# Joining the attention result by transfers and a GpSimd addition, with one low half fewer per other block, in a fused attention and two-layer kernel

## The chip, the cores and the metric

One core of one Trainium2 chip runs one program. The metric is device microseconds (us) of one execution; the figure for a kernel is the median of its runs. TensorE (PE, with PEld for its weight loads) multiplies matrices, VectorE (DVE), ScalarE (ACT) and GpSimd (POOL) work on tiles, and SyncE (SP) issues nearly all DMA transfers.

## The reference

Attention is limited by hash buckets: with B = 2, H = 8, S = 768, D = 64, a score counts only where the six sign bits of `q @ proj` and `k @ proj` agree.

```python
mask = q_bucket[:, :, :, None] == k_bucket[:, :, None, :]
scores = np.where(mask, scale * np.matmul(q, k.transpose(0, 1, 3, 2)), -1e9)
attn = np.exp(scores - np.max(scores, axis=-1, keepdims=True))
attn = attn / (np.sum(attn, axis=-1, keepdims=True) + 1e-09)
x = np.matmul(attn, v)                 # to (1536, 512)
h = x @ w_in;  g = h * np.tanh(softplus(h));  x = g @ w_out      # 512 -> 2048 -> 512
h = x @ w2_in; g = h - np.tanh(h);            out = g @ w2_out
```

## The kernel before, in words

The arithmetic is float32. For each product the kernel splits an operand into a rounded high half and a low half (value minus high) and multiplies high by high, low by high and high by low.

Every piece of work is an `op` with an engine, a modelled cost and a key. `Plan.order` simulates all of them on modelled engines (ready operations by key) and writes out one fixed order for each engine; SP's DMA issues are ordered in the same way (engine "DMA"). The chip then runs each engine's list in order, with semaphores between the engines. All constants `AT_*`, `TICK`, `JIT`, `TOK_T`, `LATG` enter keys and modelled latencies only, so they change the order and nothing else.

**Attention** takes the eight head pairs g = 0 to 7 one after the other. A pair has four blocks (head h in 0, 1; half of the queries in 0, 1), a block has three score tiles and six key chunks of 128, so a pair has 24 chunks ("ticks") and 12 score tiles. Some tiles, those with t = 2 among them, are made in two parts of 512 and 256 columns.

- `scores` (L668 to L694): PE products, a DVE clamp with minimum, an ACT exponential with a running sum.
- `chunk`: three PE transposes (L734, L736) into a PSUM tile `pt`; then ACT casts the high half `ph` (L757) and DVE subtracts for the low half `pl` (L763), or, for the chunks that `POOL_C` names ("pooled"), ACT copies to `f` (L749) and GpSimd makes both halves (L421 `ph<-f`, L753 `pl<-f,ph`). `product` (L706, L709) multiplies them with the values five chunks later (`PV_LAG`); `ph` and `pl` have `GX_BUFS` buffers.
- `gather`, at the end of each block: the PSUM accumulator `o` holds 64 rows from the high values and 64 rows from the low values. ACT copies it to `f` (L771), and DVE adds one half of its rows to the other (L774, 64x384) into `u`.
- `finish`, after the second head: GpSimd multiplies `u` by the inverse sums `r` (L822) and makes `xh` and `xl` (L421 `xh`, L829). For the last pair DVE and ACT do it.
- During a pair GpSimd also makes the next pair's q and k halves (L472 scaling, L503 low halves; ACT casts `qh`, L477) and the value halves (L627), and parts of the conversion of the first weights (`to_float`, with DVE L954 and L962, GpSimd L974).

**Token sums.** `tokens` builds block sums of the finished x. Its `diff` operations, through the helper `add` (L920), are DVE subtractions with both inputs in SBUF; those for the first batch become ready during attention.

**Port waits.** DVE and GpSimd operations that touch only SBUF are kept apart in the plan (`inside`, `LOCK`). When the order is written out, each GpSimd operation gets a wait on the last such DVE operation before it in the order:

```python
made = o.fn()
if o.eng == "DVE" and plan.inside(o) and made is not None:
    holders.append(made)
elif o.eng == "POOL" and made is not None:
    for h in holders[-1:]:
        tc.add_manual_dep(made.ins, h.ins.name, ...)
```

The helper `add` returns nothing, so an operation that goes through it is no holder.

**The two layers** (units of 256 hidden columns, with one level of Strassen-like sums) follow from about 216 us on; their first weight conversions lie under the attention.

Of the kernel before, what the change touches and what calls it, by code (L numbers as in the profile page):

```python
# [27 lines left out]
F32 = mybir.dt.float32  # L28
# [4 lines left out]
ALU = mybir.AluOpType  # L33
# [3 lines left out]
MASKED = float(2.0**60)  # L37


POOL_C = ((1, 4), (4,), (1, 4), (4,))  # L40
POOL_LAST = ((4,), (), (4,), ())
SPLIT_S = (1, 3, 5)
SPLIT_T = (2,)
TAIL = 3
WARM = 7
HOLD = 7
GUARD = 0.3
# [2 lines left out]
G2_BUFS = 4  # L50
G_BUFS, E_BUFS = 3, 3
F_BUFS = 2
GX_BUFS = 6
T_BUFS, P_BUFS, U_BUFS = 4, 3, 3
PAD = 8
CLOSE_AT = 0
RAW_BUFS = 2
RAW_LAT = 4.0
Q_SCALE = "POOL"
Q_HIGH = "ACT"  # L60
RATE, ISSUE = 250e3, 0.55
C_STORE, C_SPREAD = 1.3, 1.2
INV = 2
# [8 lines left out]
AT_F = 0.1  # L72
AT_PH = -1.5
AT_PL = 0.3
AT_H = -0.4
AT_L = 0.6
AT_PV = 0.05
AT_C = 0.1
AT_E = 0.2
AT_GA = 0.0  # L80
AT_GD = 1.0
AT_FIN = 3.0
# [1 line left out]
T_COST, T_FIRST, PV_COST = 0.222, 0.222, 0.36  # L84
LATE = 0.15
LATS = 0.1
LATG = 0.5
LAGS = {
    ("PE", "ACT"): 0.24, ("PE", "DVE"): 0.25, ("ACT", "PE"): 0.17, ("ACT", "DVE"): 0.2, ("ACT", "POOL"): 0.19,
    ("DVE", "PE"): 0.15, ("DVE", "ACT"): 0.15, ("DVE", "POOL"): 0.16, ("POOL", "PE"): 0.13, ("POOL", "DVE"): 0.15, ("POOL", "ACT"): 0.15,  # L90
# [2 lines left out]

TICK = 1.04
T_ATT = 8.0
M0 = 9.0
AHEAD = 11
PV_LAG = 5  # L100
# [5 lines left out]
FIRST = (1.0, 0.0, 1.6, 5.0)  # L106
ON_K0 = "PAP"
ON_K1 = "PPA"
ON_Q0 = "APP"
ON_Q1 = "ADP"  # L110
BY_ACT = (("q", 1),)
LAG1 = 0.35
# [6 lines left out]
UNIT = 15.6  # L119
STEP = 1.06  # L120
OUT2 = 28.0
JIT = 18.0
DGL = 0.48
DY = 0.48
LATO = 1.0
# [8 lines left out]
TOK_A = 30.0  # L134
TOK_L = 85.0
TOK_S = 0.8
TOK_T = 2.5
CONV_A = 5
CONV_S = 24
CONV_R = 15.0  # L140
# [42 lines left out]
class Plan:  # L183
# [11 lines left out]
    def buf(self, pool, tag, shape, dtype=F32):  # L195
        return Buf(self, pool, tag, shape, dtype)

    def op(self, eng, cost, key, fn, reads=(), writes=(), after=(), release=0.0, lat=None):
        o = Op()
        o.lat = (LAT_DMA if eng == "DMA" else self.LAT.get(eng, LATE)) if lat is None else lat  # L200
        o.n, o.eng, o.cost, o.key, o.fn = len(self.ops), eng, cost, key, fn
        o.deps, o.users, o.bufs = {}, [], []
        for tok in reads:
            w = self.writer.get(tok)
            if w is not None:
                o.deps[w] = True
            self.readers.setdefault(tok, []).append(o)
        for tok in writes:
            w = self.writer.get(tok)
            if w is not None:  # L210
                o.deps[w] = True
            for r in self.readers.pop(tok, ()):
                if r is not o:
                    o.deps[r] = True
            self.writer[tok] = o
        for a in after:
            o.deps.setdefault(a, False)
        for tok in (*reads, *writes):
            b = tok[0] if isinstance(tok, tuple) else tok
            if isinstance(b, Buf) and b not in o.bufs:  # L220
                o.bufs.append(b)
                b.refs += 1
                self.by_pool.setdefault(b.pool, []).append(o)
        o.wait, o.ready = len(o.deps), release
        for d in o.deps:
            d.users.append(o)
        self.ops.append(o)
        return o
# [93 lines left out]
def tile_lsh_attention_moe(  # L322
# [13 lines left out]
    nc = tc.nc  # L336
    _, P2, S = q.shape
    D = P2 // 2
    KF, P, DM = w_in1.shape
# [3 lines left out]
    NT = S // P  # L343
    NP = H // 2
    KD = DM // P
    HB = S // 2
# [10 lines left out]
    op, buf, room = plan.op, plan.buf, plan.room  # L357
# [24 lines left out]
    for name, tags, n in (*wd, *wb):  # L382
# [3 lines left out]
    prep = (("qkv", "q k v", 1), ("tqk", "qh ql kh kl", 1), ("z", "z", 1))  # L386
    core = (
        ("stack", "a b c d", 2), ("p", " ".join(f"p{i}" for i in range(P_BUFS)), 1), ("vt", "vt", 3), ("gx", "ph pl", GX_BUFS),
        ("u", "u", U_BUFS), ("r", "r", 2), ("rt", "rt", 2), ("small", "mn mn2 sums", 6),
    )  # L390
    ctx.enter_context(
        memory("left", (
# [9 lines left out]
    const, xy_p = plan.pools["const"], plan.pools["xy"]  # L402
# [4 lines left out]
    pjl = const.tile([P, NJ], F32R, name="pjl")  # L407
    idr = const.tile([P, P], F32R, name="idr")
    rds = [const.tile([P, 32], F32, name=f"rd{i}") for i in range(2)]
    const.tile([P, 78], F32, name="even")  # L410
    xh = [xy_p.tile([P, B * S], F32R, name=f"xh{kk}") for kk in range(KD)]
    xl = [xy_p.tile([P, B * S], F32R, name=f"xl{kk}") for kk in range(KD)]

# [11 lines left out]
    def dma(nbytes, key, out, in_, reads=(), writes=(), release=0.0, rate=None, lat=None):  # L425

        op("DMA", max(ISSUE, nbytes / (rate or RATE)), key, lambda: nc.sync.dma_start(out=out(), in_=in_()), reads, writes, release=release, lat=lat)
# [4 lines left out]
    n_items = len(pairs) * TICKS  # L432
    T_MOE = T_ATT + n_items * TICK + M0

    def at(tick):
        return T_ATT + tick * TICK

    raws, vts, stacks, sums, rs = {}, {}, {}, {}, {}
# [20 lines left out]
    def halves_split(g, nm, halves, key):  # L459
# [4 lines left out]
        for i in halves:  # L464
            c = slice(i * HB, (i + 1) * HB)
            k0 = key + 0.2 * i
            if nm == "q" and g:
                if Q_SCALE == "ACT":
                    op("ACT", 0.42, k0 - 0.1, lambda c=c: nc.scalar.activation(out=raw()[:, c], in_=raw()[:, c], func=AF.Copy, scale=-SCALE), [], [(raw, i)])
                else:  # L470
# [4 lines left out]
                    )  # L475
                if Q_HIGH == "ACT":
                    op("ACT", 0.42, k0, lambda c=c: nc.scalar.copy(th()[:, c], raw()[:, c]), [(raw, i)], [(th, i)])  # L477
# [105 lines left out]
    def first_stack(half, nm, key):  # L583
# [9 lines left out]
        engs = {"A": act_op, "P": pool_op, "D": dve_op}  # L593
        todo = [(engs[e], dst, rows, x, top) for e, (dst, rows, x) in zip({"k": (ON_K0, ON_K1), "q": (ON_Q0, ON_Q1)}[nm][half], dsts)]
        for (eng, cost, f), dst, rows, src, from_ in todo:
# [56 lines left out]
    def scores(g, h, half, t, key, p, after):  # L652
# [34 lines left out]
        else:  # L687
# [4 lines left out]
        return op(  # L692
            "ACT", 0.945, key + AT_E,
            lambda: nc.scalar.activation(  # L694
# [24 lines left out]
    queue, spent = [], []  # L719

    def chunk(g, h, half, c, ps, o, key, done):

        vt = vts[g, h]
        kind = POOL_LAST if g == len(pairs) - 1 else POOL_C
        pooled = c in kind[((2 * g + h) * 2 + half) % len(kind)]
# [21 lines left out]
        if pooled:  # L747
            pf = buf("f", "f", [P, XB])
            op("ACT", 0.38, key + AT_F, lambda: nc.scalar.copy(pf()[:, w], pt()[:, :HB]), both, [pf])  # L749
            op("POOL", 0.48, key + AT_PH, lambda: pool_copy(ph()[:, w], pf()[:, w]), [pf], [ph], lat=LATG)  # L750
            op(
                "POOL", 0.95, key + AT_PL,
                lambda: nc.gpsimd.tensor_tensor(out=pl()[:, w], in0=pf()[:, w], in1=ph()[:, w], op=ALU.subtract),  # L753
                [pf, ph], [pl], lat=LATG,
            )
        else:
            op("ACT", 0.376, key + AT_H, lambda: nc.scalar.copy(ph()[:, w], pt()[:, :HB]), both, [ph])  # L757
            old = spent.pop() if c == CLOSE_AT and spent else None
# [6 lines left out]
            op("DVE", 0.49 if old else 0.47, key + AT_L, low, [*both, ph], [pl, *((old, t) for t in range(TB) if old)])  # L765
        queue.append((vt, c, ph, pl, o, done))

    def gather(h, o, u, key):
        main, rest = slice(h * D, (h + 1) * D), slice((1 - h) * D, (2 - h) * D)
        tt = buf("f", "f", [P, XB])  # L770
        op("ACT", 0.38, key + AT_GA, lambda: nc.scalar.copy(tt()[:, :HB], o()[:, :HB]), [o], [tt])  # L771
        op(
            "DVE", 0.55, key + AT_GD,
            lambda: nc.vector.tensor_tensor(  # L774
                out=u()[main, :HB], in0=o()[main, :HB], in1=tt()[rest, :HB], op=ALU.add
            ),
            [o, tt], [(u, h)],
        )
# [66 lines left out]
    for g in range(len(pairs)):  # L845
        load(g)
        k0 = at(TICKS * (g - 1)) if g else 0.0
        if g == 0:
            clear_stack()
        else:  # L850
            for n, nm in enumerate("kq"):
                halves_split(g, nm, (0, 1), k0 + PIECE * n * TICK)
        if g:
            for half in range(2):
                hash_bits(g, half, k0 + (BITS + 2 * half) * TICK)
        else:
            for key, (nm, half) in zip(FIRST, (("k", 0), ("q", 0), ("k", 1), ("q", 1))):
                halves_split(0, nm, (half,), key)
                first_piece(nm, half, key)
                first_stack(half, nm, key + LAG1)  # L860
        for h in range(2):
            if g or h:
                stack(g, h, k0 + STACK * TICK if g else 5.0)
            values_in(g, h, k0 + (VALUES + 2 * h) * TICK)
        us = []
        sums[g] = buf("small", "sums", [P, 2 * TB, 4])
        for half in range(2):
            us.append(kept_x(g, half))
        for h in range(2):
            for half in range(2):  # L870
                n = (2 * g + h) * 2 + half
                ps, before = Weights(n), []
                for t in range(TB):
                    before = [scores(g, h, half, t, at(NT * n + 2 * t - AHEAD) + 0.3, ps, before)]
                o = buf("ps_t", "pt", [P, 512]) if n else opened[0]
                if h == 1 and half == 1:
                    inverse(g, at(NT * n - INV))

                def done(g=g, h=h, half=half, o=o, u=us[half], key=at(NT * (n + 1)) + PV_LAG):
                    gather(h, o, u, key)  # L880
                    if h == 1:
                        finish(g, half, u, key + AT_FIN)

                for c in range(NT):
                    chunk(g, h, half, c, ps, o, at(NT * n + c), done if c == NT - 1 else None)
                spent.append(ps)
# [30 lines left out]
    dram = {}  # L917

    def add(eng, out, in0, in1, sub=False):
        eng.tensor_tensor(out=out, in0=in0, in1=in1, op=ALU.subtract if sub else ALU.add)  # L920

    def unit_at(n):
        return T_MOE + n * UNIT
# [141 lines left out]
    def unit_weights(layer, sb, u, plain):  # L1065
        n = number(layer, sb, u)
        odd = n % 2
        key = unit_at(n) - JIT
        gate = ["wd"] if odd else ["wb"]
# [469 lines left out]
    for rd in rds:  # L1539
        nc.vector.memset(rd, 0.0)  # L1540
    for _ in range(WARM):
        o = plan.pools["ps_t"].tile([P, XB], F32, tag="pt", name="hot_ps")
# [71 lines left out]
```

## Time and profile before

| | us |
|---|---|
| median of 3 runs | 739.85 (739.48 to 739.94) |
| the profiled execution | 739.25 |
| its span, first to last instruction | 737.5 |
| busy in the span: PE, DVE, ACT, POOL | 717.1, 647.6, 508.8, 181.8 |

Busy times are unions of instruction intervals. Neighbouring intervals of a pipelined engine overlap, so the pitch from one start to the next is the time that an instruction takes from its engine. POOL works in the first 230 us alone.

### The profile page before, as it was taken

How to read it: one execution, taken by the hardware profiler on the slowest of the kernel's cores; microseconds unless marked ns; L12 is line 12 of the kernel's file. 1: busy time of each engine (PE TensorE's matmuls, PEld its weight loads, DVE VectorE, ACT ScalarE, POOL GpSimd, SP SyncE). 2: the span in 40 equal slices, each digit the busy share in tenths (PEclk: the TensorE clock that was granted, in tenths of full speed). 3: DMA queues.
4: the chain of work that ended last, by engine and by line, in shares of the span. 5: the costliest groups of instructions: out<-in, count | busy, mean ns of one | idle time of the engine just before them, and what ended most of it. 6: DMA issues, size and time to landing. Idle time of an engine off the chain costs nothing.

```text
span 737.5 us, 12852 instructions
## 1 busy us (share of the span) xinstructions
PE 717.1 (97%) x4381; PEld 656.0 (89%) x4381; DVE 647.6 (88%) x1348; ACT 508.8 (69%) x1093; POOL 181.8 (25%) x245
## 2 busy tenths in 40 slices
PE   8995999999999999999999999999999999999998
PEld 5784898888888998999999999999999899999998
DVE  7999999999999999998798998789999575767883
ACT  5994898999995966676576666676666345476660
POOL 6797599989950000000000000000000000000000
PEclk9997999999999999999999999999999999999999
DMA  8884568686651665556544754999876786745621
GB/s 216 201 219 113 151 171 211 171 217 170 135 186 25 232 194 172 175 198 224 205 171 144 253 208 174 363 362 326 326 282 251 279 272 241 229 156 189 212 97 64
DMA packets 60673, 150.87 MB, mean 205 GB/s; under 512 B 7256, under 2 KB 23768, under 8 KB 60608
## 3 DMA queue, kind: packets, MB, share of 16 engines
q1 hardware_dynamic: 60320, 149.75, 62.8%
q8 instruction: 34, 0.56, 0.3%
q10 hardware_dynamic: 288, 0.30, 0.2%
q14 instruction: 31, 0.25, 0.1%
HBM read 88.19 MB, written 43.04 MB: 178 GB/s over the span
## 4 chain that ended last, share of the span: by engine, by line
PE 73%; DVE 17%; issue 4%; ACT 3%; POOL 1%; DMA 1%; SPq 0%; DVEq 0%; POOLq 0%; ACTq 0%
PE pt L1152 10%; PE pt L1154 10%; PE pt L1153 10%; PE pt L1242 6%; DVE p L672 6%; PE pt L1230 5%; PE pt L1229 5%; PE s L1229 5%; PE pt L1468 5%; PE s L1468 3%; PE s L1242 3%; DVE pl L763 2%; PE pt L736 2%; PE pt L709 2%; PE pt L706 2%
## 5 line engine op out<-in xcount | busy, mean ns | idle before, releaser
L694 ACT ACTIVATE p<-p,mn 128x768 f32<-128x768 f32 x96 | 91.1, 949 | 17.8 <-DVE p L672 15.9
L1152 PE MATMUL pt<-xh,a 128*128 128x384 f32 x280 | 94.3, 337 | 0.4 <-DVE ph L920 0.4
L1154 PE MATMUL pt<-xh,a 128*128 128x384 f32 x280 | 94.4, 337 | 0.0
L1153 PE MATMUL pt<-xl,a 128*128 128x384 f32 x280 | 94.4, 337 | 0.0
L763 DVE TENSOR_TENSOR pl<-pt,ph 128x384 fp32r<-128x384 f32 x148 | 77.4, 548 | 1.2 <-ACT ph L757 0.2
L757 ACT CAST ph<-pt 128x384 fp32r<-128x384 f32 x148 | 68.2, 486 | 8.0 <-PE pt L736 6.4
L1230 PE MATMUL pt<-gh,o 128*128 128x256 f32 x256 | 71.9, 281 | 0.0
L736 PE MATMUL pt<-idr,split 128*128 128x128 f32 x544 | 68.6, 241 | 0.2 <-DVE pl L763 0.2
L736 PEld LDWEIGHTS pt<-idr,split 128*128 128x128 f32 x544 | 62.3, 141 | 5.7 <-DVE p L672 0.4
L709 PE MATMUL pt<-pl,vt 128*64 128x384 f32 x192 | 66.2, 348 | 0.1
L706 PE MATMUL pt<-ph,vt 128*128 128x384 f32 x192 | 66.0, 345 | 0.0
L920 DVE TENSOR_TENSOR gl<-pl,gh 128x384 fp32r<-128x384 f32 x96 | 52.4, 553 | 10.1 <-ACT gh L1176 9.8
L672 DVE TENSOR_SCALAR_CACHE_REDUCE p<-s 128x768 f32<-128x768 f32 x62 | 58.7, 947 | 2.1 <-PE s L669 1.9
L668 PE MATMUL s<-b,a 128*128 128x512 f32 x124 | 45.5, 367 | 11.2 <-DVE p L672 10.9
L1152 PEld LDWEIGHTS pt<-xh,a 128*128 128x128 f32 x280 | 52.6, 188 | 3.8 <-DVE ph L920 0.7
L1153 PEld LDWEIGHTS pt<-xl,a 128*128 128x128 f32 x280 | 52.6, 188 | 1.2
L1154 PEld LDWEIGHTS pt<-xh,a 128*128 128x128 f32 x280 | 52.5, 188 | 0.0
L1176 ACT CAST gh<-pl 128x384 fp32r<-128x384 f32 x96 | 48.7, 514 | 4.7 <-DVE pl L920 3.8
L1190 ACT COPY ph<-pt 128x384 f32<-128x384 f32 x58 | 27.9, 482 | 32.7 <-PE pt L1154 32.6
L1230 PEld LDWEIGHTS pt<-gh,o 128*128 128x128 f32 x256 | 48.1, 188 | 0.0
L1229 PE MATMUL s<-gh,o 128*128 128x512 f32 x128 | 47.6, 394 | 0.0
L1229 PE MATMUL pt<-gh,o 128*128 128x512 f32 x128 | 47.6, 394 | 0.0
(333 smaller groups left out, 2149.1 us busy)
## 6 DMA issues: line engine op xcount, KB each, us to landing
w<-w SPq DMA_DIRECT2D x52, 512.0 KB
raw<-in_moe_w_in_dram SPq DMA_DIRECT2D x14, 1024.0 KB
raw<-in_moe_w_out_dram SPq DMA_DIRECT2D x14, 1024.0 KB
split<-a SPq DMA_DIRECT2D x24, 512.0 KB
a<-split SPq DMA_DIRECT2D x24, 512.0 KB
w<-raw SPq DMA_DIRECT2D x16, 512.0 KB
o<-split SPq DMA_DIRECT2D x24, 256.0 KB
b<-kh SPq DMA_DIRECT2D x30, 192.0 KB
```

The source lines that it names most:

```text
L672: nc.vector.tensor_scalar(out=out, in0=in_, scalar1=MASKED, scalar2=first, op0=ALU.min, op1=ALU.min, accum_out=low)
L694: lambda: nc.scalar.activation(out=p.tile(t), in_=p.tile(t), func=AF.Exp, bias=mn(), scale=-1.0, accum_out=sm()[:, st, h:h + 1],),
L706: nc.tensor.matmul(o()[:, :HB], vt()[:, c, :], ph()[:, :HB], start=(c == 0), stop=(c == NT - 1), skip_group_check=True)
L709: nc.tensor.matmul(o()[:D, :HB], vt()[:, c, :D], pl()[:, :HB], start=False, stop=False, skip_group_check=True)
L736: nc.tensor.transpose(pt()[:, t * P:(t + 1) * P].bitcast(F32R), ps.turned(t, c), idr)
L757: op("ACT", 0.376, key + AT_H, lambda: nc.scalar.copy(ph()[:, w], pt()[:, :HB]), both, [ph])
L763: nc.vector.tensor_tensor(out=pl()[:, w], in0=pt()[:, :HB], in1=ph()[:, w], op=ALU.subtract)
L1152: nc.tensor.matmul(o, tl()[:, 0, c], at_(0, kk), start=start and kk == 0, stop=False, skip_group_check=not start)
L1153: nc.tensor.matmul(o, tl()[:, 0, c], at_(1, kk), start=False, stop=False, skip_group_check=not start)
L1154: nc.tensor.matmul(o, tl()[:, 1, c], at_(0, kk), start=False, stop=kk == 1, skip_group_check=not start)
L1229: nc.tensor.matmul(a()[:, n, :], w()[:, y, c], flat[x][:, :SEG], start=st, stop=sp)
L1230: nc.tensor.matmul(r()[:, 0, rest], w()[:, y, c], flat[x][:, SEG:], start=st and d % 2 == 0, stop=sp, skip_group_check=True)
```

## The change

For pairs 0 to 6 (`g < EXCHANGE`), `gather` is replaced by `exchange`. The first head's `o` is copied by ACT to `u`, and one transfer moves its lower 64 rows to the upper rows of a new tile `lows`. The second head's `o` is copied by ACT to a new tile `tt`; two transfers move its upper rows to the lower rows of `lows` and its lower rows to the lower rows of `u`. GpSimd then adds `lows` to `u` over all 128 rows at once. The last pair keeps `gather`.

Blocks with two pooled chunks, (1, 4), get one, (4,); the last pair's list stays. The high half of q is cast by GpSimd instead of ACT (`Q_HIGH`). `ph` and `pl` get five buffers instead of six. `add` returns its instruction, so its DVE operations become holders for the port waits. Three small copies of the first pair's q move between engines (`ON_Q0`: ACT, POOL, POOL becomes DVE, ACT, ACT). The remaining lines change keys and modelled latencies.

```diff
-POOL_C = ((1, 4), (4,), (1, 4), (4,))
+POOL_C = ((4,), (4,), (4,), (4,))
+EXCHANGE = 7
-GX_BUFS = 6
+GX_BUFS = 5
-Q_HIGH = "ACT"
+Q_HIGH = "POOL"
-AT_H = -0.4
+AT_H = 0.5
-AT_E = 0.2
+AT_E = -0.4
-LATG = 0.5
+LATG = 0.2
-TICK = 1.04
+TICK = 1.0
-ON_Q0 = "APP"
+ON_Q0 = "DAA"
-JIT = 18.0
+JIT = 16.0
-TOK_T = 2.5
+TOK_T = 3.4
...
-        ("u", "u", U_BUFS), ("r", "r", 2), ("rt", "rt", 2), ("small", "mn mn2 sums", 6),
+        ("u", "u", U_BUFS), ("r", "r", 2), ("rt", "rt", 2), ("lows", "lows", 2), ("tt", "tt", 1), ("small", "mn mn2 sums", 6),
...
-    const.tile([P, 78], F32, name="even")
...
+    def exchange(h, o, u, lows, key):
+        top, rest = slice(0, D), slice(D, 2 * D)
+        if not h:
+            op("ACT", 0.38, key + AT_GA, lambda: nc.scalar.copy(u()[:, :HB], o()[:, :HB]), [o], [(u, 0), (u, 1)])
+            dma(D * HB * 4, key + 0.3, lambda: lows()[top], lambda: u()[rest, :HB], [(u, 1)], [(lows, 0)])
+            return
+        tt = buf("tt", "tt", [P, HB])
+        op("ACT", 0.38, key + AT_GA, lambda: nc.scalar.copy(tt(), o()[:, :HB]), [o], [tt])
+        dma(D * HB * 4, key + 0.3, lambda: lows()[rest], lambda: tt()[top], [tt], [(lows, 1)])
+        dma(D * HB * 4, key + 0.31, lambda: u()[rest, :HB], lambda: tt()[rest], [tt], [(u, 1)])
+        op(
+            "POOL", 0.975, key + AT_GD,
+            lambda: nc.gpsimd.tensor_tensor(out=u()[:, :HB], in0=u()[:, :HB], in1=lows(), op=ALU.add),
+            [(lows, 0), (lows, 1)], [(u, 0), (u, 1)],
+        )
...
-                    gather(h, o, u, key)
+                    if lows[half] is None:
+                        gather(h, o, u, key)
+                    else:
+                        exchange(h, o, u, lows[half], key)
...
     def add(eng, out, in0, in1, sub=False):
-        eng.tensor_tensor(out=out, in0=in0, in1=in1, op=ALU.subtract if sub else ALU.add)
+        return eng.tensor_tensor(out=out, in0=in0, in1=in1, op=ALU.subtract if sub else ALU.add)
```

## Rows read from the trace of the kernel before

**Rows 1.** Windows: start:end, length, then busy us of PE, PEld, DVE, ACT, POOL; clock, DMA.
```profile
10.00:60.00 50.00, 47.84 (x318) 40.27 (x318) 48.66 (x124) 42.69 (x97) 41.21 (x54) 1.00 0.81 204
60.00:66.00 6.00, 1.98 (x17) 1.54 (x15) 5.98 (x2) 2.11 (x7) 6.00 (x9) 0.96 0.90 201
66.00:72.00 6.00, 1.42 (x4) 1.23 (x5) 5.59 (x6) 1.40 (x3) 3.23 (x5) 0.50 0.12 48
...
280.00:430.00 150.00, 149.59 (x854) 139.10 (x853) 136.13 (x243) 101.53 (x199) 0.00 (x0) 1.00 0.56 197
```

**Rows 2.** Timeline of DVE around 60 us: start us, us, engine, line, operation.
```profile
60.49 9.15 DVE L920 TENSOR_TENSOR pl<-ph,pl 128x384 f32<-128x384 f32 x1
69.57 0.95 DVE L672 TENSOR_SCALAR_CACHE_REDUCE p<-s 128x768 f32<-128x768 f32 x1
```

**Rows 3.** Timeline of POOL over the same time.
```profile
60.78 1.29 POOL L974 TENSOR_TENSOR w<-w,raw 128x512 uint32<-128x512 uint32 x1
62.05 0.98 POOL L421 TENSOR_SCALAR ph<-f 128x384 fp32r<-128x384 f32 x2
63.00 0.98 POOL L753 TENSOR_TENSOR pl<-f,ph 128x384 fp32r<-128x384 f32 x1
...
67.30 1.93 POOL L503 TENSOR_TENSOR kl<-k,kh 128x384 fp32r<-128x384 f32 x2
```

**Rows 4.** Waits from 55 to 75 us: who waited for whom, total, times, longest.
```profile
PE s L668 <- DVE p L672: 8.6, 1, 8.6
```

**Rows 5.** Windows by pair, between the L774 additions of each pair's first block.
```profile
59.42:95.59 36.17, 27.57 (x180) 24.29 (x179) 33.92 (x66) 23.91 (x58) 23.30 (x32) 0.86 0.51 128
95.59:121.99 26.40, 25.98 (x181) 22.33 (x180) 26.08 (x65) 24.26 (x57) 25.34 (x34) 1.00 0.78 211
121.99:147.35 25.36, 24.89 (x181) 22.16 (x180) 24.68 (x65) 23.91 (x57) 23.73 (x32) 1.00 0.68 171
147.35:172.58 25.23, 25.18 (x179) 21.80 (x178) 24.83 (x63) 23.50 (x55) 23.13 (x31) 1.00 0.80 213
172.58:198.94 26.36, 25.60 (x185) 22.73 (x184) 25.97 (x67) 24.96 (x58) 24.23 (x32) 1.00 0.57 134
```

**Rows 6.** Timeline of DVE: a gather addition, a low half, another `diff`, a clamp.
```profile
147.35 0.55 DVE L774 TENSOR_TENSOR u<-pt,f 64x384 f32<-64x384 f32 x1
147.84 0.07 DVE L650 MEMSET split<- 128x8 f32 x1
147.95 0.56 DVE L763 TENSOR_TENSOR pl<-pt,ph 128x384 fp32r<-128x384 f32 x1
148.43 1.48 DVE L920 TENSOR_TENSOR ph<-ph 128x384 f32<-128x384 f32 x1
```

**Rows 7.** Timeline of PE: start of a score tile and its end, start of a chunk and its end.
```profile
157.20 0.40 PE L668 MATMUL s<-b,a 128*128 128x512 f32 x1
...
157.93 0.28 PE L668 MATMUL pt<-b,a 128*128 128x256 f32 x1
...
158.41 0.36 PE L709 MATMUL pt<-pl,vt 128*64 128x384 f32 x1
...
158.99 0.35 PE L709 MATMUL pt<-pl,vt 128*64 128x384 f32 x1
```

**Rows 8.** Timeline of PE: first of the six hash products of a half, and what follows them.
```profile
21.51 0.35 PE L516 MATMUL pt<-qh,pjh 128*56 128x384 f32 x1 [0.72 <-DVE p L672]
...
22.57 0.39 PE L668 MATMUL s<-b,a 128*128 128x512 f32 x1
```

**Rows 9.** Waits of POOL on DVE `w`, 76 to 215 us: first and last of six.
```profile
POOL xl L829 <- DVE w L962: 1.1, 1, 1.1
...
POOL kl L503 <- DVE w L954: 0.4, 1, 0.4
```

**Rows 10.** The chain that ended last: its one transfer between 100 and 160 us.
```profile
126.63 2.39 DMA c<-z
```

More of the change, by code (lines that the diff above doesn't have):

```diff
@@ L864, in tile_lsh_attention_moe @@
             values_in(g, h, k0 + (VALUES + 2 * h) * TICK)
-        us = []
+        us, lows = [], [buf("lows", "lows", [P, HB]) if g < EXCHANGE else None for _ in range(2)]
         sums[g] = buf("small", "sums", [P, 2 * TB, 4])
@@ L877, in tile_lsh_attention_moe, with done @@
                     inverse(g, at(NT * n - INV))
-                def done(g=g, h=h, half=half, o=o, u=us[half], key=at(NT * (n + 1)) + PV_LAG):
-                    gather(h, o, u, key)
+                def done(g=g, h=h, half=half, o=o, lows=lows, u=us[half], key=at(NT * (n + 1)) + PV_LAG):
+                    if lows[half] is None:
+                        gather(h, o, u, key)
+                    else:
+                        exchange(h, o, u, lows[half], key)
                     if h == 1:
```

## The prediction

> **What bounds the kernel now.** I read the windows by stage first. In the two layers PE is busy 149.59 of 150 us [rows 1], and the change puts nothing into their arithmetic, so nothing is to be had there. The attention is left. At first sight it is as full: PE 47.84 of 50 us, DVE 48.66. Then come twelve microseconds in which PE works 1.98 and 1.42 of 6 us, while DVE counts as busy throughout [rows 1].
>
> The timeline of DVE names the cause. One `diff` subtraction, both inputs in SBUF, starts at 60.49 and lasts 9.15 us; the next DVE instruction starts at 69.57 [rows 2]. POOL in that time works through its list without a gap, from the 1.29 us conversion at 60.78 to two low halves that end at 69.23 [rows 3]. The same kind of `diff` takes 1.48 us at 148.43 [rows 6]. So the 9 us are no work; DVE was kept out until POOL paused. The waits show the price: PE stood 8.6 us for the clamp behind that subtraction [rows 4]. When PE came back the granted clock was 0.50, the lower of its two levels, 1.2 GHz [rows 1].
>
> The windows by pair give the whole cost and the normal pace. The four undisturbed pairs take 26.40, 25.36, 25.23 and 26.36 us, mean 25.84; the pair with the stall takes 36.17 [rows 5]. The stall with its slow clock costs 36.17 - 25.84 = 10.3 us.
>
> What sets 25.84? Busy means over the four are DVE 25.4, PE 25.4 (its intervals overlap), POOL 24.1, ACT 24.2 [rows 5]. DVE, at 98%, with starts that follow one another, is first, and nobody is far behind. PE's own floor comes from pitches: a chunk 0.58 (158.41 to 158.99), a score tile 0.73 (157.20 to 157.93) [rows 7], the hash products of a half 1.06 [rows 8]; 24 x 0.58 + 12 x 0.73 + 2 x 1.06 = 24.8 us a pair.
>
> **Port waits.** `add` now returns its instruction, so the `diff` operations become holders, and the next POOL operation in the order waits until the subtraction is done. A `diff` then can be late by what POOL still has ahead of it. The 1.48 us example is 0.9 above the 0.55 of an unhindered addition of that width [rows 6]; I allow 0.3, inside 0 to 0.9. Removed: 10.3 - 0.3 = **10.0 us** (bounds 9.4 to 10.3). The new waits hold POOL's queue, and with it the halves of the next q and k and the pooled low halves, for a subtraction's 0.55 us each time; the two `diff` operations shown lie 88 us, more than three pairs, apart, others lie between, and I allow half of one, 0.3, a pair.
>
> Beside this stands a rule of the Trainium skill, "SBUF — State Buffer", section "SBUF: two separate sides": a DVE instruction with two SBUF inputs and a GpSimd instruction that reads SBUF exclude each other through a shared port pair, and whoever starts first has it for the whole instruction. By that rule the subtraction would have got in after one POOL instruction, at 62.07 at the latest; the row shows 69.6, so here the measurement decides, and one instruction's grace is not what DVE got. Taken strictly the rule says the 9 us have another cause and that waits on POOL remove nothing; that is the rival "stall stays" below, near 735.
>
> **DVE.** Four gather additions a pair leave it, 0.49 each by their pitch (147.35 to 147.84); two low halves come, 0.48 each (147.95 to 148.43) [rows 6]. Net -4 x 0.49 + 2 x 0.48 = -1.0 us: 25.84 becomes 24.8.
>
> **POOL.** Two pooled chunks leave: 0.48 for the high half (two in 0.95) and 0.97 for the low half (two in 1.93) [rows 3], -2.9. Two casts of q come, taken at the same 0.48: +0.96. Two additions of 128x384 come, taken at 0.97: +1.94. Sum 0.0. POOL stays at 24.1 a pair of work. To it come its waits on DVE's conversions, six in 139 us, 1.1 down to 0.4, together 3.9, or 0.7 a pair [rows 9], and the 0.3 from above: 25.1. So POOL, not DVE, becomes the slowest list, and 25.84 - 25.1 = **0.74 us a pair** is what I count. ACT loses two casts a pair, is not first, and gives nothing.
>
> Only pairs 0 to 5 carry the full POOL load (the seventh prepares the last, whose finish is elsewhere, and overlaps the layers' start), so 6 x 0.74 = **4.4 us**. Bounds: nothing, if POOL's added waits eat it; 7 x (25.84 - 24.8) = 7.3, if POOL's finishing work is put off and PE's floor decides.
>
> **Transfers.** Six more a pair on SP's queue, 42 in all. What they carry is needed by POOL's addition, one block after the first head's and directly for the second. The trace has no such transfer; the nearest is the 2.39 us that the chain waited for `c<-z` [rows 10]. Behind the waiting addition stand POOL's finish, next pair's halves and the pooled low halves, and PE waits for the last. From 0, if the order puts other POOL work into the gap, to 2.39 for each of 14 additions. I take 0: POOL has 25.84 - 24.1 = 1.7 us a pair without work now, and the order has other POOL work to put there. The far end is a rival.
>
> **The rest.** Five buffers for `ph`, `pl`: the cast of a chunk now needs the product five chunks back, which PE issues right behind the transposes. From 0 to the whole relief of DVE (then DVE waits again and the pair stays at 25.84, rival two); I take 0, since DVE is the list with room. `ON_Q0` moves three copies once, before the first score; at GpSimd's 0.48 a copy [rows 3] that is within 0.5 either way, and I take 0. Keys and latencies: their effect in the layers is bounded by the 0.4 us in 150 that PE stands [rows 1] on the gain side and I allow 1 us for loss; their effect in the attention is inside the two bounds of the pair.
>
> **Sum.** The profiled execution, 739.25, stands 0.6 below the median, 739.85. 739.25 - 10.0 - 4.4 = 724.85, and with the 0.6: **725.4**.
>
> **Rivals.**
> *Stall gone, no relief.* POOL at 25.1 plus small transfer waits leaves the pair at 25.84. For it: POOL's 24.1 of 25.84 [rows 5]. Against: DVE, which was first, loses 1.0. 739.85 - 10.0 = 729.9.
> *PE's floor.* POOL puts off its finishing work and 24.8 decides: 739.85 - 10.3 - 7.3 = 722.2. Against: DVE stands at 24.8 as well, and three lists at one level do not mesh without loss.
> *Stall stays.* Another DVE operation is kept out by a POOL that runs late, or the 9 us were not POOL's doing: 739.85 - 4.4 = 735.4. Against: the subtraction ended within 0.5 us of POOL's pause [rows 2, 3].
> *Slower: POOL stands for transfers.* Each of its two additions a pair waits w in order. 1.7 us a pair are free; to give back 10.0 over seven pairs takes another 1.4, so it decides from w = 1.6 us on. At 2.39 [rows 10] the pair grows by 4.8 - 1.7 = 3.1, and 739.85 - 10.0 + 7 x 3.1 = 751.5. For it: 2.39 is above 1.6. Against: the order leaves a modelled latency before the addition and fills it with other work.
>
> **How the numbers follow.** Forecast (723.5 to 728) 0.50; no relief (728 to 732) 0.22; PE's floor (720.5 to 723.5) 0.14; stall stays 0.06; slower 0.05; mishaps that end within 0.2% of 739.85, about what a measurement can tell from no change, 0.03. The likeliest gives 725.4. 720.5 to 732.5 holds the first three, 0.86, less their edges. Faster by over 0.2%: 0.50 + 0.22 + 0.14 + 0.06 = 0.92; same 0.03; slower 0.05.
>
> **What would show it.** No `diff` above some 1.5 us in the timeline of DVE, and granted clock 1.00 in every window after the start; pairs of about 25.1 us, with DVE below 97% busy and POOL's idle time mostly waits on DVE; POOL additions that start without a wait on a transfer. Wrong would be: a pair above 25.84, a POOL wait on `lows` above 1.6 us in most pairs, or a second long DVE instruction.

## The result

| | us |
|---|---|
| median after, 6 runs | 730.78 (727.98 to 734.17) |
| median before, beside it, 6 runs | 739.74 (738.77 to 741.5) |
| ratio | 0.9878, 95% interval 0.9847 to 0.9909 |
| the profiled execution after, its span | 727.98, 726.1 |

The change is 1.2% faster. The prediction was 725.4 with a range of 720.5 to 732.5: sign and range hold, but the time is that of the rival "stall gone, no relief" (729.9). One thing is needed to read later numbers: single runs of the kernel before, 69 beside the experiments, lie at 738.2 to 741.8 in 51 cases and at 728.6 to 730.8 in the other 18, so its median is that of the more frequent time.

The page of the changed kernel, busy time and PE, POOL and clock in 40 slices; no slice of PE between the first and the last is below 9, and the clock stays up:

```profile
PE 713.5 (98%) x4381; PEld 653.9 (90%) x4381; DVE 631.9 (87%) x1335; ACT 502.4 (69%) x1080; POOL 183.5 (25%) x243
...
PE   7999999999999999999999999999999999999998
...
PEclk9999999999999999999999999999999999999999
```

The timeline of DVE, the first three `diff` subtractions (L940 is the line of `add` now). The first took 9.15 us before [rows 2], the third is of the kind that took 1.48 [rows 6]:

```profile
59.52 0.85 DVE L940 TENSOR_TENSOR pl<-ph,pl 128x384 f32<-128x384 f32 x1 [0.27 <-POOL ph L839]
...
92.90 0.93 DVE L940 TENSOR_TENSOR t<-t 128x384 f32<-128x384 f32 x1
...
110.40 0.94 DVE L940 TENSOR_TENSOR ph<-ph 128x384 f32<-128x384 f32 x1
```

Windows by pair, here from the first transposes of one pair to those of the next:

```profile
43.66:68.67 25.01, 25.01 (x182) 22.45 (x181) 23.83 (x63) 23.02 (x55) 23.47 (x30) 1.00 0.83 211
68.67:94.47 25.80, 25.39 (x182) 22.57 (x181) 24.40 (x64) 23.15 (x56) 22.90 (x31) 1.00 0.83 201
94.47:120.71 26.24, 25.38 (x182) 22.27 (x181) 24.23 (x64) 22.74 (x55) 24.39 (x33) 1.00 0.85 220
120.71:146.13 25.42, 25.39 (x181) 22.28 (x180) 25.16 (x64) 22.66 (x54) 22.72 (x31) 1.00 0.74 190
146.13:171.31 25.18, 25.14 (x183) 22.50 (x182) 24.59 (x64) 23.65 (x57) 23.67 (x30) 1.00 0.87 227
171.31:197.89 26.58, 25.86 (x184) 22.82 (x183) 25.97 (x66) 23.60 (x57) 23.00 (x29) 1.00 0.78 194
```

The pair of 36 us is gone. The others are as long as before: mean 25.70 here, 25.84 in [rows 5], where 25.1 was forecast; two of the six stand above 25.84, which the prediction had named as a sign of being wrong. So the stall was removed and the relief is missing. DVE is busy for less of each pair than before (24.7 of 25.7 us against 25.4 of 25.84), and PE is not faster.

### The profile page after: what moved, and what is told of

It is laid out like the page before. It is cut to its first block, busy times and chain, and to the rows that moved or that the text cites. A ratio compares the mean times of both kernels' runs of the same rounds, so it can differ in the third digit from the quotient of the medians.

```text
span 726.1 us, 12930 instructions
## 1 busy us (share of the span) xinstructions
PE 713.5 (98%) x4381; PEld 653.9 (90%) x4381; DVE 631.9 (87%) x1335; ACT 502.4 (69%) x1080; POOL 183.5 (25%) x243
## 4 chain that ended last, share of the span: by engine, by line
PE 85%; DVE 5%; DMA 4%; ACT 2%; SPq 1%; issue 1%; POOL 1%; DVEq 0%; POOLq 0%; ACTq 0%
PE pt L1172 10%; PE pt L1174 10%; PE pt L1173 10%; PE pt L1262 6%; PE pt L1250 6%; PE s L1249 6%; PE pt L1249 5%; PE pt L1488 5%; PE pt L736 4%; PE pt L709 4%; PE pt L706 4%; PE s L1488 3%; PE s L1262 3%; PE s L668 2%; PE s L669 2%; SPq L427 1%
## 5 line engine op out<-in xcount | busy, mean ns | idle before, releaser
L1172 PE MATMUL pt<-xh,a 128*128 128x384 f32 x280 | 94.8, 339 | 0.2 <-DVE ph L940 0.2
L763 DVE TENSOR_TENSOR pl<-pt,ph 128x384 fp32r<-128x384 f32 x162 | 84.7, 547 | 1.5 <-ACT ph L757 0.7
L757 ACT CAST ph<-pt 128x384 fp32r<-128x384 f32 x162 | 75.2, 484 | 9.9 <-PE pt L706 6.6
L706 PE MATMUL pt<-ph,vt 128*128 128x384 f32 x192 | 66.1, 346 | 1.4 <-DVE pl L763 1.4
L940 DVE TENSOR_TENSOR gl<-pl,gh 128x384 fp32r<-128x384 f32 x96 | 52.2, 551 | 8.5 <-ACT gh L1196 8.1
L1172 PEld LDWEIGHTS pt<-xh,a 128*128 128x128 f32 x280 | 52.6, 188 | 3.7 <-DVE ph L940 0.6
L940 DVE TENSOR_TENSOR o<-w,o 128x512 fp32r<-128x512 f32 (+1 forms) x68 | 40.5, 606 | 5.9 <-ACT o L1138 4.7
```

The costliest lines, as they stand in the source:

```text
L706: nc.tensor.matmul(o()[:, :HB], vt()[:, c, :], ph()[:, :HB], start=(c == 0), stop=(c == NT - 1), skip_group_check=True)
L763: nc.vector.tensor_tensor(out=pl()[:, w], in0=pt()[:, :HB], in1=ph()[:, w], op=ALU.subtract)
L940: return eng.tensor_tensor(out=out, in0=in0, in1=in1, op=ALU.subtract if sub else ALU.add)
L1172: nc.tensor.matmul(o, tl()[:, 0, c], at_(0, kk), start=start and kk == 0, stop=False, skip_group_check=not start)
```

## The experiments

Every edit that touches an operation lets the plan order all engines anew, so such an experiment measures the edit with the new order that comes with it. The edits of the wait and of the width of a product leave all orders as they were. Where the time of each profile lies helps to tell the two apart. The marks are the starts of the first transposes (L734, a line later in some runs) of the second and of the last pair, in us:

| profile | up to the second pair | six pairs | last pair and layers |
|---|---|---|---|
| kernel before | 43.8 | 165.9 | 527.8 |
| one-line kernel (1) | 44.2 | 155.1 | 527.8 |
| changed kernel, first profile | 43.7 | 154.2 | 528.3 |
| changed kernel, second profile (4) | 44.6 | 157.3 | 529.0 |
| without the return (2) | 43.9 | 161.2 | 529.2 |
| gather (5) | 45.0 | 157.6 | 531.9 |
| old list of pooled chunks (5) | 45.3 | 168.2 | 528.7 |
| transfers doubled (6) | 43.8 | 173.9 | 532.5 |
| shorter product, changed kernel (7) | 45.1 | 154.2 | 527.2 |
| transfers issued by ACT (8) | 45.5 | 163.6 | 534.7 |
| direct copy (8) | 43.9 | 155.4 | 533.2 |

The layers start later than the "about 216 us" given above: their first product (L1152, in the changed kernel L1172) stands at 231.9 us in the kernel before, 221.6 in the one-line kernel and 219.7 in the first profile after.

**1. The return alone, in the kernel before.**

```diff
-        eng.tensor_tensor(out=out, in0=in0, in1=in1, op=ALU.subtract if sub else ALU.add)
+        return eng.tensor_tensor(out=out, in0=in0, in1=in1, op=ALU.subtract if sub else ALU.add)
```

> The kernel before with one edit: the helper add returns its instruction, so that three more GpSimd operations wait on a DVE subtraction (the orders of all engines stay the same). Theory (DVE is kept out until GpSimd pauses, and the wait makes the pause): the 9.15 us subtraction becomes 1.5 us or less and the time falls by 9 to 11 us, to 729 to 731, which is all that the whole change gained. Rival (the 9 us are not GpSimd's doing, or the exchange brings the gain): 739 to 740, the long instruction stays.

Median of 12 runs 729.01 (728.52 to 730.9), the kernel before beside it 739.67; the ratio, 0.9932 (0.9885 to 0.9979), is taken over a mixture of that kernel's two times. The one line takes off 10.7 us and leaves only the times that the kernel before has in its rarer case. Its timeline:

```profile
60.94 0.71 DVE L920 TENSOR_TENSOR pl<-ph,pl 128x384 f32<-128x384 f32 x1
...
61.73 1.31 POOL L974 TENSOR_TENSOR w<-w,raw 128x512 uint32<-128x512 uint32 x1 [0.49 <-DVE pl L920]
```

GpSimd's conversion now waits 0.49 us for the subtraction, and the subtraction takes 0.71. The pair with the stall falls from 36.3 to 26.0 us, and the other five stay within 0.5 us of what they were. This is the whole gain of the change and more.

**2. The changed kernel without the return.**

> The changed kernel without the return in add (everything else of the change stays). Theory (the wait is what protects the subtractions, wherever they fall): those subtractions that GpSimd work follows without a pause grow, one or more of them to several us, and the time rises above the changed kernel's by about what they grow. Rival (the new order alone moves them out of harm's way): the same time as the changed kernel, 728 to 734, no subtraction above 2 us.

736.04 (734.63 to 737.1; 6 runs). The stall is back at another place, in the timeline of DVE and POOL:

```profile
93.39 6.17 DVE L940 TENSOR_TENSOR t<-t 128x384 f32<-128x384 f32 x1
...
97.21 1.93 POOL L503 TENSOR_TENSOR ql<-q,qh 128x384 fp32r<-128x384 f32 x2
```

6.17 us instead of 0.93, 5.4 us in the time. It ends at 99.56, just after GpSimd's unbroken run of work ends (99.14). The other five subtractions up to 200 us took 0.60 to 1.34 us without any wait. So the new order alone does not protect all of them, and one miss is enough to cost the 5.4 us.

**3. The wait placed further back.** `SKIP` GpSimd operations behind a subtraction pass without the wait, the next one gets it; first in the kernel before (4), then in the changed one (3).

```diff
+            if by_add and by_add[-1] is made:
+                late.append([made, SKIP])
...
+            for x in late:
+                x[1] -= 1
+            held += [x[0] for x in late if x[1] < 0][-1:]
```

> The kernel before with the new wait put on the fifth GpSimd operation behind the subtraction instead of on the next one. Theory (DVE gets in when GpSimd pauses, not when one GpSimd instruction ends): the subtraction at about 60.5 us lasts until the fourth of them has ended, 1.29 + 2 x 0.48 + 0.97 = 3.2 us and some tenths. Rival (whoever comes first has the port for one instruction): about 1 us, as with the next one.

One run, 730.44, and it tells nothing about the theory, because here DVE was not kept out at all (timeline of POOL and DVE; L979 is the conversion, L473 the scaling):

```profile
61.12 1.00 POOL L473 TENSOR_SCALAR q<-q 128x384 f32<-128x384 f32 x2
...
61.81 0.71 DVE L923 TENSOR_TENSOR pl<-ph,pl 128x384 f32<-128x384 f32 x1
...
62.08 1.60 POOL L979 TENSOR_TENSOR w<-w,raw 128x512 uint32<-128x512 uint32 x1
```

DVE started 0.27 us before the next GpSimd instruction, got in at that boundary, and the conversion took 1.60 us instead of 1.29. In [rows 2, 3] it started 0.29 us before the same boundary and was kept out for the next 8.5 us. The lead does not decide it, though: in other places DVE got in with leads up to 0.91 us (last section). This run's 730.44 lies in the lower group of the kernel before, so a boundary that is won or lost from run to run would explain its two times. No run of the lower group of that kernel has a trace, so this is inferred.

> The changed kernel with the wait for the subtractions put on the fourth GpSimd operation behind each instead of on the next; without any such wait the subtraction t<-t at 93.4 us took 6.17 us in every sign that the times gave. Theory (DVE gets in when GpSimd pauses): this subtraction lasts until the third operation behind it has ended, 0.46 + 0.48 + 0.97 + 0.97 and some tenths, 2.8 to 3.4 us. Rival (one instruction's grace): 0.9 us. A wait that far behind that does not help: 6 us.

In the changed kernel, where this boundary was lost in both profiles (this one and that of experiment 2), it worked as a measurement:

```profile
94.76 3.35 DVE L943 TENSOR_TENSOR t<-t 128x384 f32<-128x384 f32 x1
...
95.25 0.51 POOL L422 TENSOR_SCALAR ph<-f 128x384 fp32r<-128x384 f32 x1
95.73 1.01 POOL L504 TENSOR_TENSOR kl<-k,kh 128x384 fp32r<-128x384 f32 x1
96.70 0.99 POOL L754 TENSOR_TENSOR pl<-f,ph 128x384 fp32r<-128x384 f32 x1
98.20 0.99 POOL L422 TENSOR_SCALAR qh<-q 128x384 fp32r<-128x384 f32 x2 [0.50 <-DVE t L943]
```

3.35 us: DVE got in when the third operation had ended (97.7) and the fourth stood for it. Time 733.09 (731.69 to 733.77). With the wait on the next, on the fourth and on no operation the subtraction takes 0.93, 3.35 and 6.17 us.

**4. The changed kernel again.**

> The changed kernel once more, for the spread of its runs (728 to 734 the first time) and a second profile. If the spread comes from a wait that depends on the timing of transfers, the pairs of blocks with transfers in their chain differ between the two profiles and the pairs whose chain is PE alone do not; if it comes from the layers, the time after 215 us differs.

730.65 (728.61 to 732.92; 12 runs), beside 729.01 of the one-line kernel on the same chip: all the rest of the change costs 1.6 us. The second profile is of an execution of 732.72. Windows from 45 to 200 us of the one-line kernel, of the first profile after and of the second:

```profile
45.00:200.00 155.00, 152.40 (x1081) 134.11 (x1080) 152.28 (x390) 144.72 (x338) 140.10 (x181) 1.00 0.71 183
```
```profile
45.00:200.00 155.00, 152.93 (x1092) 135.61 (x1090) 148.95 (x384) 139.59 (x329) 140.15 (x179) 1.00 0.81 206
```
```profile
45.00:200.00 155.00, 151.39 (x1070) 132.63 (x1069) 146.59 (x375) 136.89 (x321) 140.21 (x178) 1.00 0.81 202
```

DVE's busy time falls from 152.28 to 148.95 and 146.59: the relief is there, and it has become idle time. What took its place is seen in the waits over the same stretch. The one-line kernel, all that the view lists for the `ph` cast and for DVE:

```profile
ACT ph L757 <- PE pt L736: 2.6, 6, 0.6
...
DVE p L672 <- PE s L669: 0.3, 1, 0.3
```

The first profile after:

```profile
ACT ph L757 <- PE pt L706: 5.6, 11, 1.0
DVE p L672 <- PE s L669: 3.7, 9, 0.8
...
ACT tt L776 <- DMA ph<-tt: 0.9, 1, 0.9
...
POOL qh L421 <- DMA inv<-rt: 0.7, 1, 0.7
```

The second profile:

```profile
ACT ph L757 <- PE pt L706: 4.0, 10, 0.6
DVE p L672 <- PE s L669: 3.5, 8, 0.8
POOL kh L421 <- DMA c<-qh: 2.2, 1, 2.2
...
ACT tt L776 <- DMA t<-tt: 1.8, 2, 1.2
...
ACT tt L776 <- DMA ph<-tt: 1.6, 1, 1.6
...
POOL qh L421 <- DMA c<-qh: 1.1, 1, 1.1
POOL t L781 <- DMA lows<-tt: 1.1, 1, 1.1
```

Three kinds of wait are new or have grown. DVE's clamp waits for PE's score tiles, 3.5 to 3.7 us instead of 0.3. The cast of a chunk waits for the product L706 five chunks back, 4 to 5.6 us in ten or eleven places; the step from six buffers to five makes this wait possible, but does not set its size alone, since the kernel with gather and five buffers (5) shows 1.9 us of it in three places. And ACT and GpSimd wait for transfers: 1.6 us in the first profile, 7.8 in the rows shown of the second, whose execution was 4.7 us longer.

The expectation asked which pairs differ between the two profiles. Of the three whose chain was PE nearly alone in the first, two are the same (25.01 and 24.96, 25.18 and 25.16) and one is not (25.42 and 27.48). Those with other work in their chain are 25.80 and 26.39, 26.24 and 26.33, 26.58 and 26.98. The pair that grew by 2.1 begins behind a wait of GpSimd for a transfer:

```profile
119.82 0.99 POOL L421 TENSOR_SCALAR kh<-k 128x384 fp32r<-128x384 f32 x2 [2.16 <-DMA c<-qh]
```

Its chain goes on through the late low halves of k and q to PE. So the spread goes with the waits on transfers, as far as two profiles can tell; 0.7 of the 4.7 us lies behind the six pairs.

In the pair before the last (171 to 198 us of the first profile) the chain that ended last leaves the engines, its shares by line and three of its pieces:

```profile
by line: SPq L427 24.0%; DMA b<-kh 11.7%; DMA c<-z 10.3%; ACT p L694 6.1%; DVE w L974 5.7%; issue 5.6%; ACT ph L757 5.1%; PE pt L736 5.0%; PE pt L709 4.2%; PE pt L706 4.2%; PE s L668 3.6%; DVE p L672 3.3%; PE pt L669 2.7%; PE s L669 2.7%; P
...
176.55 3.16 DMA b<-kh
179.72 1.55 DVE w L974
...
191.09 2.78 DMA c<-z
```

SP issues one transfer after the other there; those of the exchange come before those that fill the score operands (`b<-kh`, `c<-z`), which land later. That GpSimd then overwrites `kh` late and DVE meets a late GpSimd is the reading of this chain, not a test of it.

**5. Gather in place of the exchange; the old list of pooled chunks.** Two parts of the change undone, one at a time, in the changed kernel.

```diff
-EXCHANGE = 7
+EXCHANGE = 0
```

> The changed kernel with gather in all pairs: no transfers and no GpSimd addition, DVE adds again; the waits, the single pooled chunk and all keys of the change stay. If the exchange is worth its DVE time (DVE was the bound): DVE gets 4 x 0.49 = 2.0 us a pair back on top of the two low halves, 26 a pair, and the time rises to 734 to 740. Rival (with the stall gone PE's floor of about 25 us and the transfers decide, so that the exchange only trades one for another): 728 to 732, the same as the changed kernel.

736.71 (735.13 to 739.65): 6.1 above the changed kernel, less than half of the 14 us of DVE time that the exchange saves (7 x 2.0). The table above shows that not all of it is the exchange's: the six pairs are 3.3 us longer than in the first profile after, but only 0.3 longer than in the second, while the last pair, which gathers in both kernels, and the layers take 2.9 to 3.6 us more. That part came with the new order. So the exchange pays something within this kernel; how much is not shown.

The wait of the cast for the product, in this kernel with five buffers:

```profile
ACT ph L757 <- PE pt L706: 1.9, 3, 0.7
```

```diff
-POOL_C = ((4,), (4,), (4,), (4,))
+POOL_C = ((1, 4), (4,), (1, 4), (4,))
```

> The changed kernel with the list of pooled chunks of before, six a pair instead of four: GpSimd gets 2.9 us a pair more (27 a pair), DVE 1.0 less. If GpSimd is the bound that took the place of DVE, the time rises by about 2.9 x 6 = 17 us, or at least by 5. Rival (PE decides and GpSimd has room): within 2 us of the changed kernel.

744.0 (742.66 to 746.47): 13.4 above, with GpSimd busy for 149.42 of 155 us in the windows:

```profile
45.00:200.00 155.00, 147.74 (x998) 125.75 (x997) 135.49 (x342) 128.85 (x299) 149.42 (x192) 0.99 0.76 192
```

GpSimd is the bound there. 2.9 us more a pair lengthen the time by 13.4 / 7 = 1.9 a pair, so about 1 us a pair of it was free. The exchange and the fewer pooled chunks belong together: the one fills GpSimd with what the other empties.

**6. The transfers doubled.**

```diff
+            again(key, lambda: u()[rest, :HB], [(u, 1)])
...
+        again(key, lambda: tt()[top], [tt])
+        again(key, lambda: tt()[rest], [tt])
```

> The changed kernel with a second transfer beside each of the 42 of the exchange, of the same source and size, to a place in memory that nobody reads: six more issues a pair on SP's queue and their share of the DMA engines. If the loaded queue is what eats the relief, the time rises by 3 us or more and the spread of the runs grows. Rival (SP and the transfers have room): within 1 us of the changed kernel.

751.98 (750.34 to 753.87): 21.3 above, half a microsecond for each of 42 transfers that nobody reads, most of it in the six pairs; the spread of the runs did not grow. The waits (40 to 215 us), among them GpSimd's scaling on the load of the next q:

```profile
ACT p L694 <- DVE p L672: 16.9, 19, 2.6
POOL q L472 <- DMA q<-in_q_dram: 10.3, 4, 3.6
ACT ph L757 <- PE pt L706: 9.6, 11, 2.0
```

Added transfers are far from free, then. That SP's queue is full is not shown: its issues take 111 us of the six pairs' 155 in the one-line kernel, 135 of 154 in the first profile after and 146 of 174 here, so it stands still for a sixth of the time, and the DMA engines are busy for a share of 0.79, against 0.81 there. How much of the 21.3 us is SP's issue time, the transfers themselves or the order that was planned around them stays open.

**7. PE's work shortened**, with all orders as they were, in the changed and in the one-line kernel.

```diff
-            nc.tensor.matmul(o()[:D, :HB], vt()[:, c, :D], pl()[:, :HB], start=False, stop=False, skip_group_check=True)
+            nc.tensor.matmul(o()[:D, :P], vt()[:, c, :D], pl()[:, :P], start=False, stop=False, skip_group_check=True)
```

> The changed kernel with the low product of every chunk over 128 of its 384 columns (the low values of two thirds of the queries are left out); all orders stay. PE loses about 0.12 us a chunk, 2.9 a pair, and nothing else changes. Theory (with the stall gone PE's own 25 us a pair is the bound of most pairs): the time falls by 3 us or more, to 722 to 728. Rival (GpSimd, the transfers and DVE decide in all pairs): less than 1 us.

730.9 (726.86 to 732.38): nothing. The test is half as strong as was expected, because the next product takes back a part of what the low product saves. A low product, a high one and the transposes behind them, in the first profile after and in this one:

```profile
160.41 0.35 PE L709 MATMUL pt<-pl,vt 128*64 128x384 f32 x1
160.60 0.34 PE L706 MATMUL pt<-ph,vt 128*128 128x384 f32 x1
160.78 0.37 PE L736 MATMUL pt<-idr,split 128*128 128x128 f32 x3
```
```profile
150.05 0.24 PE L709 MATMUL pt<-pl,vt 128*64 128x128 f32 x1
150.13 0.39 PE L706 MATMUL pt<-ph,vt 128*128 128x384 f32 x1
150.36 0.37 PE L736 MATMUL pt<-idr,split 128*128 128x128 f32 x3
```

From the first start to the third it is 0.37 and 0.31 us, so PE loses 0.06 a chunk, 1.4 a pair. Had PE decided in most pairs, the time would still have fallen by several us (six pairs at 1.4 are 8.4). It did not, and the theory that PE's floor had become the bound of most pairs falls. It was read from the first profile, where the chain of three pairs is PE nearly alone (25.01, 25.42 and 25.18 us); with less PE work the chain of 45 to 200 us is nobody's:

```profile
by line: issue 10.2%; DVE p L672 7.7%; SPq L427 6.6%; ACT p L694 6.5%; PE pt L706 6.4%; ACT ph L757 5.3%; PE s L668 5.1%; PE s L669 4.3%; PE pt L736 4.3%; POOL pl L753 3.8%; DVE pl L763 3.7%; DMA c<-z 3.0%; DMA t<-tt 2.7%; PE pt L709 2.5%; 
```

> The same shortening in the kernel before with the one-line wait. There DVE's instructions follow one another without a gap, so that PE's shorter work should give little: under 2 us below 729.0. If it gives as much as in the changed kernel, PE decided there too and DVE's relief could bring nothing from the start.

727.53 (726.46 to 727.99): 1.5 less, inside the expected 2, as of a stretch that DVE leads.

**8. Two ways to take load off SP.** First the exchange's transfers issued by ACT, then one transfer less for each second head, ACT copying its lower rows straight into `u`.

```diff
-        dma(D * HB * 4, key + 0.31, lambda: u()[rest, :HB], lambda: tt()[rest], [tt], [(u, 1)])
+        op("ACT", 0.4, key + 0.31, lambda: nc.scalar.dma_start(out=u()[rest, :HB], in_=tt()[rest]), [tt], [(u, 1)], lat=3.0)
```

> The changed kernel with the 42 transfers of the exchange issued by ACT instead of SP, at 0.4 us of ACT each (2.4 a pair). If SP's issue time is what the 42 transfers cost, pairs whose chain ran through SP get shorter and the time falls by 1 to 4 us. Rival (it is the transfers themselves, or ACT at 23 + 2.4 us a pair becomes the bound): the same or slower.

746.86 (745.07 to 750.32), 16.2 above.

```diff
-        dma(D * HB * 4, key + 0.31, lambda: u()[rest, :HB], lambda: tt()[rest], [tt], [(u, 1)])
+        op("ACT", 0.38, key + AT_GA + 0.01, lambda: nc.scalar.copy(u()[rest, :HB], o()[rest, :HB]), [o], [(u, 1)])
```

> The changed kernel with one transfer less per block of the second head: ACT copies the lower 64 rows of the accumulator straight into u (same rows, no transfer needed), the upper rows into tt, in two copies instead of one. Four transfers a pair instead of six, ACT 0.9 us a pair more. The doubled transfers cost 0.5 us each; if the existing ones cost a part of that, the 14 saved give 1 to 5 us and the spread of the runs shrinks: 726 to 729.5. Rival (the existing 42 are hidden): 730 to 732.

735.88 (734.16 to 740.35), 5.2 above and over the rival's 730 to 732, with a larger spread and not a smaller one. Neither prices SP. With the direct copy the six pairs take 155.4 us, no more than in the changed kernel (154.2 and 157.3); the loss is in the last pair and the layers, 4 to 5 us, where the order was planned anew too. With ACT as the issuer the six pairs lose 6.3 to 9.3 us and the rest 5.7 to 6.5. An issue took ACT 0.47 us in the median; how much of the loss in the pairs is that and how much the order is not shown.

**The version that beats both** is the kernel before with the one line: 729.01 against 730.65 of the changed kernel and 739.67 of the kernel before, on one chip.

## Why the prediction was right and wrong

**The stall: right.** Its cause was read from the timelines, its price (10.3) from the windows by pair, and 10.0 was counted. The one line alone gave 10.7. The rival "stall stays" falls, and with it the strict reading of the rule on the port: once DVE has missed the first boundary, the wait's place sets the length of the subtraction.

**The relief: wrong.** The 4.4 us did not come; the rest of the change costs 1.6. The step that failed is "25.84 - 25.1 = 0.74 us a pair is what I count", and in it the three zeros beside it.
- *DVE's term* was right in kind: net -1.0 a pair was forecast, 3.3 to 5.7 us less in the 155 us of the windows, about six pairs, were measured, and became idle time.
- *Five buffers, "I take 0, since DVE is the list with room"*: the cast waits 4 to 5.6 us for the product, where the one-line kernel shows no such wait. The other end had been written down ("the whole relief of DVE"). Whether these waits ate the relief is not shown: with gather the same five buffers gave 1.9 us of them, a kernel with six buffers beside the exchange was not tried, and neither was one with a second `tt`.
- *Transfers, "I take 0"*: POOL's additions mostly found their data, as hoped (waits of 2.6 us in the second profile, none in the first). I priced the six transfers a pair by who waits for them alone, and not by who stands behind them in SP's queue, whose issues rose from 111 to 135 us in the six pairs. The doubled transfers show that more of them cost much; what the 42 themselves cost no run shows.
- *POOL at 24.1*: right in that its work did not change (140.1 of 155 us in both kernels), and the old list shows how little was left.
- *Keys*: PE stands 0.6 us in the layers from 200 to 300 us after the last transposes in the first profile and 1.2 in the second, where it stood for nothing in the one-line kernel. Last pair and layers together are 0.4 and 1.2 us longer, about the 1 us that was allowed.

So the forecast mistook the distance to the next bound. DVE, PE, ACT and POOL all stood within 2 us a pair of the 25.84 [rows 5], and taking one of them down while loading GpSimd's order and SP's queue gave nothing. The first profile shows how near it was: its six pairs take 0.9 us less than the one-line kernel's, the second's 2.2 more. Which of the new waits ate the relief is open. That the time still lies in the stated range is the stall's doing and the width of the range.

**The rivals.** "No relief" had 0.22 and came true, by other waits than POOL's alone. "PE's floor" (722.2) falls by the time itself: three pairs of one profile came near it (25.0 to 25.4 us), the rest did not. "POOL stands for transfers" falls too: in the two profiles no addition waited longer than 1.1 us for one.

## What to carry to other kernels

When DVE and GpSimd both work in SBUF and a long DVE instruction appears beside an unbroken row of GpSimd instructions, give the next GpSimd instruction a wait on it; check that helpers return what the code that adds such waits needs. Before moving work between engines, write down the distance of every list to the pace, SP's queue included, and the buffers that are given up for it: where all stand within some 7%, as here, a relief of one may be worth nothing until the others are relieved too. When an edit lets a planner order everything anew, split the time by stage before crediting the edit with the difference. When a kernel has two times, look for a boundary that is won or lost before costing anything against its median.

## What the runs showed of the hardware

A DVE subtraction with two SBUF inputs that starts beside a running GpSimd instruction either gets in when that instruction ends or, having missed that boundary, stays out over every later one until GpSimd pauses. Four traces have no wait on the next GpSimd instruction (the kernel before, both runs of experiment 3, and experiment 2); 18 such subtractions of `add` start beside a running GpSimd instruction in them before 200 us. Thirteen were done some 0.4 us after that instruction ended, and the GpSimd instruction behind it took about 0.3 us longer, as here in experiment 2 (0.82 instead of 0.51):

```profile
137.01 1.34 DVE L940 TENSOR_TENSOR ph<-ph,pl 128x384 f32<-128x384 f32 x1
...
137.90 0.82 POOL L421 TENSOR_SCALAR xh<-t 128x384 fp32r<-128x384 f32 x1
```

Five missed it, and each was done some 0.4 us after GpSimd's next pause began: 1.48 us [rows 6] and 1.50 us with a pause one instruction later, 9.15 us over a run that ended at 69.23, 6.17 us over one that ended at 99.14, and 3.35 us where a wait was set at 97.7. The start does not tell which it will be: the thirteen started 0.11 to 0.91 us ahead of the next GpSimd instruction, the five 0.29 to 0.59. What decides at the first boundary is open.

The Trainium skill, "SBUF — State Buffer", section "Who interferes with whom", says that issue order decides who blocks and that the loser waits for the whole instruction. The thirteen agree with it; the five waited for more than one instruction, in [rows 3] for eleven (from 60.78 on), and the measurement decides.
